# A searched task order replaced by another one in a fused delta-rule attention and gated FFN kernel

## The chip, the core and the metric

The kernel runs on one core of one Trainium2 chip. The metric is the device time of one launch in microseconds (us). PE is TensorE, which multiplies matrices; DVE is VectorE, ACT is ScalarE, POOL is GpSimd, SP is SyncE. SP and ACT also issue DMA transfers, each to a queue of its own (q1 and q10 in the profile).

## What is computed

The reference is a delta-rule recurrence over 768 steps for 4 batches and 8 heads of width 48, and behind it a gated FFN on the 3072 tokens that it gives:

```python
for t in range(S):
    y[:, :, t] = einsum('bhd,bhde->bhe', q[:, :, t], state)
    v_old = einsum('bhde,bhd->bhe', state, k_n[:, :, t])
    state = state + bt * einsum('bhd,bhe->bhde', k_n[:, :, t], vt - v_old)
h = x @ w_in          # (3072, 384) @ (384, 2048)
out = (h * cos(h)) @ w_out
```

All data is 32-bit float; `k_n` is `k` over its norm.

## The kernel before

**Units.** The 768 steps are cut into 24 units of 32 steps (`unit(n)`, L1492). A unit turns its keys and queries (`turn`, L635), multiplies them into Gram matrices (`gram`, L662), inverts a triangular matrix, reads the state (`through_state`, L915, task `state`), solves (`solve`, L984), updates the state (`update`, L1019), adds what lies within the unit (`within`, L1037), and transposes the result into FFN features (`features`, L1070). Each of these is a run of small matmuls on PE with a copy, product or sum on DVE or ACT behind it (`turn_out`, `gram_keys`, `right_side`, `solve_out`, `update_out`, `within_out`, `features_out`). The state chains unit to unit.

**Inverses.** For units 0 and 1 the inverse is made by doubling (`doubling`, L1463): six levels of small matmuls on PE for each of two parities (`double(n, level, par)`, L749), with a transpose, a sum or a copy on DVE or ACT between levels. Units 2 and up go in pairs `m = n // 2`: the Gram matrix is written to DRAM (`gram_put`), read back in another layout (`gram_get`), inverted column by column on POOL (`invert`, L867, seven tasks `inv(m, 0..6)`, five shorter ones for `m = 1`, of which the first runs on DVE), written again (`put`) and read back (`get`). A `get` of units 2 and 3 is eight transfers (L900), a later one four (L908).

**FFN.** Two units make a pass `p` of 256 tokens. Passes 0 and 1 run plain: eight blocks `hidden(p, f)` (L1092) and eight output blocks `out(p, i, k)` (L1292) on PE. Passes 2 to 11 run a scheme with fewer products: 20 `layer` blocks (L1267) and 14 `out` blocks (L1349) each. The weights come as 28 transfers (`weights(t)`) and pass ACT (`split`), DVE (`shift`) and POOL (`add`) before PE can use them: `hidden(0, 0)` needs `add` 0 to 2, `hidden(0, 6)` up to 11, `out(0, 0, k)` up to `add` 15 + 4k.

**Filler.** `keep_warm` (L491) is one matmul on constants whose result nothing reads. Five run ahead of everything (`WARM_FIRST`), `WARMS` more are tasks of the order. Once `out(0, 0, 0)` has been issued, L492 lets the rest issue nothing.

**The order.** Every piece is a task, given to `order.add` with its engine, its predecessors and the buffers that it takes and gives back. `Order.LINE` (L101) is one fixed sequence over all tasks, by number in the order in which they were added; `Order.run` (L219) emits them in that sequence and hands out buffers as it goes. Each engine runs its own tasks strictly in this order (L1904 to L1910), and the transfers of SP and ACT are issued in this order across both queues (L1911 to L1915). The set `Order.OTHER` (L62) picks, task by task, the other queue (L375) or the other engine (L378): a transfer in the set goes to ACT's queue and not to SP's; an `x_sum` or `inv` in it runs on DVE and not on POOL, and a `left`, `right` or `in_sums` in it on POOL and not on DVE.

Of the kernel before, what the change touches and what calls it, by code (L numbers as in the profile page):

```python
# [59 lines left out]
class Order:  # L60

    OTHER = {  # L62
        ('gram_put', 2), ('q', 3), ('gram_get', 1), ('inv', 1, 0), ('put', 1), ('gram_put',
        4), ('gram_put', 5), ('v', 7), ('v', 8), ('v', 9), ('blocks', 11, 1), ('gram_put',
        11), ('put', 5), ('v', 13), ('put', 6), ('gram_put', 15), ('gram_get', 7), ('get',
        15), ('v', 16), ('blocks', 16, 0), ('blocks', 16, 1), ('gram_put', 16), ('blocks',
        18, 1), ('k', 19), ('blocks', 19, 0), ('gram_get', 9), ('get', 19), ('gram_put',
        20), ('v', 21), ('gram_put', 21), ('put', 10), ('gram_put', 22), ('v', 23),
        ('gram_put', 23), ('gram_get', 11), ('right', 4, 4), ('left', 1, 1, 0), ('left', 1,
        3, 0), ('left', 1, 3, 1), ('store', 1, 0), ('x_sum', 2, 'd'), ('x_sum', 2, 'n'),  # L70
        ('x_sum', 2, 'm'), ('x_sum', 2, 'e'), ('x_sum', 2, 'k'), ('x_sum', 2, 'g'),
        ('x_sum', 2, 'i'), ('x_sum', 2, 'l'), ('x_sum', 2, 'f'), ('x_sum', 2, 'b0'),
        ('left', 2, 4, 1), ('left', 2, 3, 1), ('x_sum', 3, 'd'), ('x_sum', 3, 'n'),
        ('x_sum', 3, 'm'), ('x_sum', 3, 'e'), ('x_sum', 3, 'k'), ('x_sum', 3, 'g'),
        ('x_sum', 3, 'i'), ('x_sum', 3, 'l'), ('x_sum', 3, 'h'), ('x_sum', 3, 'b0'),
        ('left', 3, 4, 1), ('left', 3, 3, 1), ('x_sum', 4, 'd'), ('x_sum', 4, 'm'),
        ('x_sum', 4, 'g'), ('x_sum', 4, 'i'), ('left', 4, 3, 0), ('left', 4, 3, 1),
        ('store', 4, 0), ('x_sum', 5, 'd'), ('x_sum', 5, 'e'), ('x_sum', 5, 'l'), ('x_sum',
        5, 'h'), ('x_sum', 5, 'b0'), ('left', 5, 2, 0), ('left', 5, 4, 1), ('left', 5, 3,
        0), ('left', 5, 3, 1), ('store', 5, 0), ('x_sum', 6, 'd'), ('x_sum', 6, 'g'),  # L80
        ('x_sum', 6, 'l'), ('x_sum', 6, 'f'), ('x_sum', 6, 'b0'), ('left', 6, 1, 0),
        ('left', 6, 4, 0), ('store', 6, 1), ('x_sum', 7, 'd'), ('x_sum', 7, 'm'), ('x_sum',
        7, 'g'), ('x_sum', 7, 'i'), ('x_sum', 7, 'f'), ('x_sum', 7, 'h'), ('x_sum', 7,
        'b0'), ('left', 7, 4, 0), ('left', 7, 4, 1), ('left', 7, 3, 1), ('x_sum', 8, 'd'),
        ('x_sum', 8, 'm'), ('x_sum', 8, 'e'), ('x_sum', 8, 'k'), ('x_sum', 8, 'g'),
        ('x_sum', 8, 'l'), ('left', 8, 3, 0), ('store', 8, 0), ('store', 8, 1), ('x_sum', 9,
        'd'), ('x_sum', 9, 'm'), ('x_sum', 9, 'e'), ('x_sum', 9, 'k'), ('x_sum', 9, 'i'),
        ('x_sum', 9, 'l'), ('x_sum', 9, 'b0'), ('left', 9, 1, 0), ('left', 9, 2, 0),
        ('left', 9, 1, 1), ('left', 9, 3, 0), ('store', 9, 0), ('x_sum', 10, 'k'), ('x_sum',
        10, 'i'), ('x_sum', 10, 'l'), ('x_sum', 10, 'h'), ('x_sum', 10, 'b0'), ('left', 10,  # L90
        1, 0), ('left', 10, 1, 1), ('left', 10, 4, 1), ('left', 10, 3, 0), ('left', 10, 3,
        1), ('store', 10, 0), ('x_sum', 11, 'd'), ('x_sum', 11, 'e'), ('x_sum', 11, 'k'),
        ('x_sum', 11, 'g'), ('x_sum', 11, 'f'), ('left', 11, 1, 0), ('left', 11, 2, 0),
        ('left', 11, 1, 1), ('left', 11, 3, 0), ('left', 11, 3, 1), ('store', 11, 1),
        ('store_right', 11), ('weights', 5), ('weights', 7), ('weights', 15), ('weights',
        16), ('weights', 18), ('weights', 20), ('weights', 22), ('weights', 23), ('weights',
        25), ('weights', 27)
    }

    WARM_FIRST, WARMS = 5, 56  # L100
    LINE = """  # L101
# [1845 lines left out]
```

## Time and profile before

| what | us |
|---|---|
| three timed runs | 638.47, 639.97, 640.19 (median 639.97) |
| profiled execution: span, first to last instruction | 636.6 |
| median of the runs less that span | 3.4 |
| PE busy, all instructions | 619.2 |
| of it `keep_warm` (L493) | 23.1 |
| DVE / ACT / POOL busy | 495.1 / 297.7 / 435.8 |

The profiled execution has no timer of its own beside its span; what lies around the span is taken to be the 3.4 us of the table. PE's records come in two per matmul (one per transpose), each with its load of the stationary operand (PEld). The profile tells by "issue" that an engine waited for nothing that the trace shows. The queue q8 carries PE's instructions in packets of 16 KB.

### The profile page before, as it was taken

The numbers are of one execution on the slowest core, as the hardware profiler recorded it, in microseconds if no ns is written. First come the engines' busy times: TensorE is split into PE (matmuls) and PEld (weight loads), VectorE is DVE, ScalarE is ACT, GpSimd is POOL, SyncE is SP. The second block draws the span as 40 slices with busy tenths as digits, with TensorE's granted clock in tenths as the row PEclk, the third lists the DMA queues.
The fourth block names the chain that finished last, engine by engine and source line by source line (L and its number), as shares of the span: only waits on it lengthen the run. The fifth ranks groups of instructions, "written<-read, shape, count | busy, mean of one in ns | idle before, by whom it ended". The sixth has DMA issues, their size and how long they took to land.

```text
span 636.6 us, 24189 instructions
## 1 busy us (share of the span) xinstructions
PE 619.2 (97%) x10176; PEld 576.2 (90%) x10176; DVE 495.1 (78%) x1030; ACT 297.7 (47%) x528; POOL 435.8 (68%) x780
## 2 busy tenths in 40 slices
PE   5999989999999999999999999999999999999997
PEld 4877877987899999999999999999999999999997
DVE  5776656779998999887898888888888776566682
ACT  3457556562423444643642644733643553545440
POOL 5247788678788788887789888886884883112241
PEclk8899999999999999999999999999999999999999
DMA  8978656563651555435435344333304102000001
GB/s 173 221 171 213 121 155 146 93 118 60 116 68 22 94 90 99 60 67 104 61 70 98 56 73 90 58 57 67 74 3 81 44 1 43 19 2 26 1 25 26
DMA packets 209381, 50.37 MB, mean 79 GB/s; under 512 B 200920, under 2 KB 204280, under 8 KB 209272
## 3 DMA queue, kind: packets, MB, share of 16 engines
q1 hardware_dynamic: 161896, 35.03, 29.3%
q10 hardware_dynamic: 47072, 13.25, 10.0%
q8 instruction: 80, 1.31, 0.9%
q0 software_dynamic: 304, 0.54, 0.4%
q14 instruction: 29, 0.24, 0.1%
HBM read 38.55 MB, written 10.22 MB: 77 GB/s over the span
## 4 chain that ended last, share of the span: by engine, by line
PE 90%; DVE 3%; DMA 3%; ACT 1%; issue 1%; POOL 0%; SPq 0%; ACTq 0%; DVEq 0%
PE p_out L1353 29%; PE p_h L1271 27%; PE p_h L1097 6%; PE p_kq L928 4%; PE p_out L1295 3%; PE p_s L1025 3%; PE p_g L673 3%; PE p_h L757 3%; PE p_kq L1055 3%; PE p_u L1000 3%; PE p_out L493 2%; PE p_h L1353 2%; PE p_z L1076 1%; DMA kp<-in_k_dram 1%; PE p_t L640 1%
## 5 line engine op out<-in xcount | busy, mean ns | idle before, releaser
L877 POOL TENSOR_TENSOR part<-z,gb 128x126 f32<-128x126 f32 (+23 forms) x321 | 144.6, 451 | 46.7 <-DMA gb<-g_dr 21.2
L884 POOL TENSOR_TENSOR z<-z,part 128x126 f32<-128x126 f32 (+23 forms) x321 | 145.5, 453 | 25.1
L1353 PE MATMUL p_out<-w_out,g_ffn 128*128 128x192 f32 x672 | 121.9, 328 | 0.3 <-DVE o L1405 0.2
L1353 PEld LDWEIGHTS p_out<-w_out,g_ffn 128*128 128x128 f32 x672 | 107.7, 190 | 1.7 <-DVE o L1405 0.7
L1150 ACT ACTIVATE turns<-turns,halfpi 128x512 f32<-128x512 f32 x96 | 68.0, 719 | 55.7 <-DVE turns L1141 42.6
L1353 PE MATMUL p_out<-w_sum,g_ffn 128*128 128x192 f32 x496 | 89.7, 329 | 0.2 <-DVE o L1405 0.2
L1271 PE MATMUL p_h<-x_sum,w_in 128*128 128x128 f32 x640 | 84.0, 277 | 0.0
L1134 ACT ACTIVATE turns<-g_ffn,quarter_turn 128x512 int32<-128x512 f32 x70 | 49.8, 719 | 66.4 <-DVE g_ffn L1288 31.3
L1353 PEld LDWEIGHTS p_out<-w_sum,g_ffn 128*128 128x128 f32 x496 | 79.6, 190 | 1.2 <-issue 0.4
L1271 PEld LDWEIGHTS p_h<-x_sum,w_in 128*128 128x128 f32 x640 | 78.8, 192 | 1.1
L1288 DVE TENSOR_TENSOR g_ffn<-g_ffn,p_h 128x512 f32<-128x512 f32 x80 | 54.3, 681 | 17.3 <-PE p_h L1271 16.4
L1141 DVE SCALAR_TENSOR_TENSOR turns<-g_ffn,turns 128x512 f32<-128x512 f32 x70 | 55.3, 796 | 13.1 <-ACT turns L1134 13.0
L1068 ACT COPY y<-p_kq 32x384 f32<-32x384 f32 x96 | 45.2, 470 | 30.4 <-PE p_kq L1055 22.5
L1153 DVE TENSOR_TENSOR g_ffn<-turns,g_ffn 128x512 f32<-128x512 f32 x70 | 51.5, 745 | 3.8 <-ACT turns L1150 3.7
L1271 PE MATMUL p_h<-x_sum,in_sum 128*128 128x128 f32 x400 | 52.9, 277 | 0.0
L572 POOL TENSOR_TENSOR knrm<-ksum,halves 128x16 f32<-128x16 f32 (+1 forms) x14 | 36.4, 2602 | 23.9 <-DMA qp<-in_q_dram 12.6
L1271 PEld LDWEIGHTS p_h<-x_sum,in_sum 128*128 128x128 f32 x400 | 49.7, 192 | 0.8
L1405 DVE SCALAR_TENSOR_TENSOR o<-p_out,o 128x192 f32<-128x192 f32 x74 | 25.1, 351 | 28.4 <-PE p_out L1353 28.0
L1097 PE MATMUL p_h<-x_ffn,w_in 128*128 128x128 f32 x384 | 45.8, 277 | 0.0
L1097 PEld LDWEIGHTS p_h<-x_ffn,w_in 128*128 128x128 f32 x384 | 44.1, 192 | 1.2
L1271 PE MATMUL p_h<-x_ffn,w_in 128*128 128x128 f32 x320 | 42.4, 277 | 0.0
L1369 POOL TENSOR_TENSOR g_ffn<-g_ffn,g_ffn 128x512 f32<-128x512 f32 x18 | 25.8, 1442 | 22.5 <-PE p_out L1353 18.7
(168 smaller groups left out, 1071.3 us busy)
## 6 DMA issues: line engine op xcount, KB each, us to landing
g_ffn<-in_moe_w_in_dram SPq DMA_DIRECT2D x10, 512.0 KB
gb<-g_dr SPq DMA_DIRECT2D x14, 256.0 KB
vp<-in_v_dram SPq DMA_DIRECT2D x68, 48.0 KB
g_ffn<-in_moe_w_out_dram SPq DMA_DIRECT2D x8, 384.0 KB
g_ffn<-in_moe_w_out_dram ACTq DMA_DIRECT2D x8, 384.0 KB
kp<-in_k_dram SPq DMA_DIRECT2D x120, 24.0 KB
out_dram<-o SPq DMA_DIRECT2D x14, 192.0 KB
zt<-z_dr SPq DMA_DIRECT2D x72, 32.0 KB
```

What stands on the lines that cost most here:

```text
L572: nc.gpsimd.tensor_tensor(out=scales[m][2][:, part], in0=sums[m, part.start][:, 0:n], in1=halves[:, 0:n], op=ALU.pow,)
L877: eng.tensor_tensor(out=part, in0=z[:, 0:rows, j, None].to_broadcast(shape), in1=a[:, j, None, j + 1 :].to_broadcast(shape), op=ALU.mult,)
L884: eng.tensor_tensor(out=behind, in0=behind, in1=part, op=ALU.subtract)
L1068: nc.scalar.copy(by_parity(y[quarter(b)]), p_kq[quarter(b ^ 1), :, b % 2])
L1097: nc.tensor.matmul(p_h[:, i], w_in[:, t, (4 * k + i) * 128 : (4 * k + i + 1) * 128], xts[p][:, t, unit * 128 : (unit + 1) * 128], start=(i ...
L1134: nc.scalar.activation(turns[p, f], hidden_of(p, f), AF.Identity, bias=quarter_turn, scale=TURN)
L1141: nc.vector.scalar_tensor_tensor(out=r, in0=hidden_of(p, f), scalar=TURN, in1=t, op0=ALU.mult, op1=ALU.subtract,)
L1150: nc.scalar.activation(r, r, AF.Sin, bias=halfpi, scale=2.0 * math.pi)
L1153: nc.vector.tensor_tensor(out=place(p, f), in0=step_of(rests.pop((p, f)), f), in1=step_of(hidden_of(p, f), f), op=ALU.mult,)
L1271: nc.tensor.matmul(p_h[:, e], in_block(*w)[:, e], x_of(p, b), start=new and e == 0, stop=True, skip_group_check=True,)
L1288: nc.vector.tensor_tensor(out=part_of(p, to), in0=part_of(p, one), in1=part_of(p, two), op=op)
L1353: nc.tensor.matmul(p_o, left(p, part, a)[:, e % 4], right(e, b), start=(e == 0), stop=(e == FT // 2 - 1), skip_group_check=True,)
```

## The change

Nothing of the work changes but its order. Three things are replaced:

```diff
     OTHER = {
-        ('gram_put', 2), ('q', 3), ('gram_get', 1), ('inv', 1, 0), ('put', 1), ('gram_put',
...
+        ('q', 3), ('v', 3), ('inv', 1, 0), ('gram_put', 5), ('gram_get', 2), ('put', 2),
...
     }
-    WARM_FIRST, WARMS = 5, 56
+    WARM_FIRST, WARMS = 5, 14
     LINE = """
-0 1 66 2 70 2084 3 71 4 8 9 72 122 67 68 5 2085 123 69 127 73 128 124 65 75 125 80 76 77 2088 178 78
...
+0 24 1 25 136 8 2 3 5 26 27 28 29 30 31 33 2042 80 81 32 4 85 86 139 137 2046 165 9 10 11 12 2050
...
```

`LINE` is new from its first row to its last. With 42 `warm` tasks fewer, a task numbered 64 or more before has a number lower by 42 after. In `OTHER`, the entries of the attention's transfers (`q`, `k`, `v`, `blocks`, `gram_put`, `gram_get`, `put`, `get`) go from 34 to 25, those of `store` from 9 to 6, those of `weights` from 10 to 11, and they are largely other ones; all `x_sum`, `left`, `right` and `inv` entries stay. So no computation changes its engine, and some transfers change between SP's and ACT's queue.

The head of PE's order, decoded (w is a `warm`, d a `double(n, level, par)`, h a `hidden`):

```
before: turn0 w w gram0 turn1 d001 d000 gram1 w d010 d100 w w d011 d110 w w w d020 w w
  d021 d101 turn2 w w d111 turn3 d030 d031 w gram2 w d120 w w d041 w w gram3 d040 w w
  d121 d050 d051 turn4 w solve0 d130 w update0 w within0 d131 d140 w features0 state1 turn5
  d141 gram4 h(0,0) d151 d150 w w solve1 w update1 within1 gram5 w h(0,2) features1 state2
  turn6 h(0,4) solve_half2 w between2 w solve2 h(0,6) update2 w within2 gram6 h(0,8)
  features2 state3 turn7 h(0,10) solve_half3 between3 solve3 out(0,0,0) h(0,12) update3
  within3 h(0,14) out(0,0,1) features3 state4 gram7 h(1,0) h(1,2) h(1,4) h(1,6) out(0,0,2)
  h(1,8) solve4
after:  w turn0 gram0 turn1 w w w w turn2 d001 d000 gram1 w w w w d101 d011 d010 gram2 d021
  d111 d020 d031 d121 turn3 d030 d100 gram3 d110 d041 d040 d131 d050 turn4 d051 d141 d120
  solve0 d130 update0 within0 d151 d140 features0 state1 d150 h(0,0) turn5 h(0,2) solve1
  update1 within1 gram4 h(0,4) gram5 state2 features1 h(0,6) turn6 h(0,8) solve_half2
  between2 out(0,0,0) solve2 update2 within2 h(0,10) state3 gram6 h(0,12) solve_half3
  between3 solve3 out(0,0,1) turn7 out(0,0,2) update3 h(0,14) features2 within3 gram7 h(1,0)
  state4 features3 h(1,2) h(1,4) h(1,6) solve4
```

The head of the order of transfers, without the first sixteen, of `k` and `q` (a = ACT's queue):

```
before: weights0 v0 weights1 k2 weights2 k3 weights3 q2 weights4 a:q3 a:weights5 k4 weights6
  v1 q4 a:weights7 k5 weights8 q5 ... a:put1 q6 a:weights16 a:gram_put5 get2 gram_get2
after:  k2 weights0 q2 weights1 k3 a:weights2 weights3 v0 weights4 k4 a:weights5 a:q3 weights6
  v1 weights7 q4 weights8 k5 a:weights9 ... put1 q6 weights17 gram_put4 weights18
  a:gram_put5 get2 weights19 a:gram_get2
```

DVE's tasks follow the same pattern: before, unit 1's doubling has three of its six levels behind it in each parity when `solve(0)` is issued; after, five levels in parity 1 and three in parity 0, and four products are left where there were six.

More of the change, by code (lines that the diff above doesn't have):

```diff
@@ L62 @@
     OTHER = {
-        ('gram_put', 2), ('q', 3), ('gram_get', 1), ('inv', 1, 0), ('put', 1), ('gram_put',
[L64 to L97, printed above, removed]
+        ('q', 3), ('v', 3), ('inv', 1, 0), ('gram_put', 5), ('gram_get', 2), ('put', 2),
+        ('get', 8), ('gram_put', 9), ('v', 10), ('gram_put', 10), ('put', 5), ('blocks', 15, 0),
@@ new lines @@
+        ('gram_put', 15), ('gram_get', 7), ('v', 16), ('gram_get', 8), ('v', 18), ('v', 19),
+        ('blocks', 19, 0), ('blocks', 20, 0), ('blocks', 20, 1), ('blocks', 22, 0),
+        ('blocks', 22, 1), ('gram_put', 22), ('gram_put', 23), ('get', 23), ('right', 4, 4),
+        ('left', 1, 1, 0), ('left', 1, 3, 0), ('left', 1, 3, 1), ('x_sum', 2, 'd'),
+        ('x_sum', 2, 'n'), ('x_sum', 2, 'm'), ('x_sum', 2, 'e'), ('x_sum', 2, 'k'),
+        ('x_sum', 2, 'g'), ('x_sum', 2, 'i'), ('x_sum', 2, 'l'), ('x_sum', 2, 'f'),
@@ new lines @@
+        ('x_sum', 2, 'b0'), ('left', 2, 4, 1), ('left', 2, 3, 1), ('x_sum', 3, 'd'),
+        ('x_sum', 3, 'n'), ('x_sum', 3, 'm'), ('x_sum', 3, 'e'), ('x_sum', 3, 'k'),
+        ('x_sum', 3, 'g'), ('x_sum', 3, 'i'), ('x_sum', 3, 'l'), ('x_sum', 3, 'h'),
+        ('x_sum', 3, 'b0'), ('left', 3, 4, 1), ('left', 3, 3, 1), ('store', 3, 1),
+        ('x_sum', 4, 'd'), ('x_sum', 4, 'm'), ('x_sum', 4, 'g'), ('x_sum', 4, 'i'),
+        ('left', 4, 3, 0), ('left', 4, 3, 1), ('store', 4, 1), ('x_sum', 5, 'd'),
@@ new lines @@
+        ('x_sum', 5, 'e'), ('x_sum', 5, 'l'), ('x_sum', 5, 'h'), ('x_sum', 5, 'b0'),
+        ('left', 5, 2, 0), ('left', 5, 4, 1), ('left', 5, 3, 0), ('left', 5, 3, 1),
+        ('x_sum', 6, 'd'), ('x_sum', 6, 'g'), ('x_sum', 6, 'l'), ('x_sum', 6, 'f'),
+        ('x_sum', 6, 'b0'), ('left', 6, 1, 0), ('left', 6, 4, 0), ('store', 6, 1),
+        ('x_sum', 7, 'd'), ('x_sum', 7, 'm'), ('x_sum', 7, 'g'), ('x_sum', 7, 'i'),
+        ('x_sum', 7, 'f'), ('x_sum', 7, 'h'), ('x_sum', 7, 'b0'), ('left', 7, 4, 0),
@@ new lines @@
+        ('left', 7, 4, 1), ('left', 7, 3, 1), ('x_sum', 8, 'd'), ('x_sum', 8, 'm'),
+        ('x_sum', 8, 'e'), ('x_sum', 8, 'k'), ('x_sum', 8, 'g'), ('x_sum', 8, 'l'),
+        ('left', 8, 3, 0), ('x_sum', 9, 'd'), ('x_sum', 9, 'm'), ('x_sum', 9, 'e'),
+        ('x_sum', 9, 'k'), ('x_sum', 9, 'i'), ('x_sum', 9, 'l'), ('x_sum', 9, 'b0'),
+        ('left', 9, 1, 0), ('left', 9, 2, 0), ('left', 9, 1, 1), ('left', 9, 3, 0),
+        ('store', 9, 0), ('x_sum', 10, 'k'), ('x_sum', 10, 'i'), ('x_sum', 10, 'l'),
```

8 lines of the change are left out of this document (added), and 196 rows, old and new, of the table LINE.

## The prediction

> **What bounds the kernel now.** The page first, then the busy time by stretch. The page's rows: the span, PE's share, PE's busy tenths in 40 slices, and the queue that carries PE's instructions.
>
> ```profile
> span 636.6 us, 24189 instructions
> PE 619.2 (97%) x10176; PEld 576.2 (90%) x10176; DVE 495.1 (78%) x1030; ACT 297.7 (47%) x528; POOL 435.8 (68%) x780
> ...
> PE   5999989999999999999999999999999999999997
> ...
> q8 instruction: 80, 1.31, 0.9%
> ```
>
> PE is the bound, but 97% hides filler. The stretches (columns: length; busy PE, PEld, DVE, ACT, POOL; clock, DMA, GB/s) are cut at events of TensorE's order:
>
> ```profile
> 14.83:45.78 30.95, 30.89 (x541) 25.12 (x542) 24.56 (x76) 14.16 (x29) 10.48 (x7) 0.90 0.84 184
> 45.78:59.05 13.27, 11.43 (x310) 9.05 (x308) 9.42 (x30) 9.05 (x19) 9.60 (x13) 1.00 0.85 230
> 59.05:79.23 20.18, 19.20 (x418) 17.34 (x412) 13.09 (x26) 13.16 (x27) 15.70 (x23) 1.00 0.67 143
> 79.23:104.64 25.41, 22.39 (x643) 18.86 (x643) 14.18 (x32) 13.47 (x26) 22.08 (x47) 1.00 0.57 147
> 104.64:632.96 528.32, 527.30 (x8184) 499.68 (x8182) 425.42 (x842) 242.27 (x419) 369.23 (x676) 1.00 0.34 61
> ```
>
> From 104.64 on PE idles 1.02 us in 528: no order of the same work can win there, it can only lose. Before, PE looks busy as well, but with what? The groups of PE between 21.3 and 104.6 us show the filler:
>
> ```profile
> L493 PE MATMUL p_out<-o 128*128 128x256 f32 x56 | 17.0, 411 | 0.0
> ```
>
> So 17 us of that stretch are matmuls that nobody reads, in places where the real work waited. The milestones of PE in the start (start, length, line, count) and behind:
>
> ```profile
> 14.88 1.97 PE L757 MATMUL p_h<-in_sum 64*64 64x64 f32 x32 [2.95 <-DVE in_sum L722]
> 33.55 1.15 PE L757 MATMUL p_h<-in_sum 64*64 64x64 f32 x32
> 47.09 1.14 PE L1000 MATMUL p_u<-vp,in_sum 64*64 64x48 f32 x32 [0.73 <-ACT kq_t L650]
> 54.45 0.55 PE L1076 MATMUL p_z<-consts,y 128*128 128x128 f32 x3 [0.46 <-ACT y L1068]
> 59.05 2.94 PE L1097 MATMUL p_h<-x_ffn,w_in 128*128 128x128 f32 x24
> 61.92 1.15 PE L757 MATMUL p_h<-w_sum 64*64 64x64 f32 x32
> ```
>
> ```profile
> 66.41 0.89 PE L1025 MATMUL p_s<-u,kp 64*64 64x96 f32 x32 [0.59 <-DVE u L1012]
> 68.54 0.86 PE L673 MATMUL p_g<-kq_t 48*32 48x64 f32 x64
> 79.89 0.88 PE L958 MATMUL p_v<-g_ffn,in_sum 32*32 32x48 f32 x64
> 81.45 0.86 PE L994 MATMUL p_u<-g_ffn,w_sum 32*32 32x48 f32 x59
> 83.87 0.28 PE L994 MATMUL p_u<-g_ffn,w_sum 32*32 32x48 f32 x5 [1.56 <-issue]
> 92.79 0.49 PE L1076 MATMUL p_z<-consts,y 128*128 128x128 f32 x3
> 101.14 0.88 PE L994 MATMUL p_u<-g_ffn,w_sum 32*32 32x48 f32 x64 [0.73 <-DVE g_ffn L978]
> ```
>
> **What the packets cost now.** 10176 matmul records and as many weight loads in 80 packets are 254 instructions each. One run of 64 small matmuls is 128 instructions in 0.8 us (79.89 to 80.70), so two runs eat a packet in under 2 us. The order puts a packet's end inside `solve(2)`, where 59 of 64 matmuls run and 1.56 us are lost on nothing that the trace names. In the window 80.9 to 82.4 us the queues show the packet that was missing, behind q1's transfers:
>
> ```profile
> q8 instruction: 1, 0.02, 5.6%
> ```
>
> From 79.89, when the packet before it was begun, to 83.87 are 3.98 us. A second place is like it, 201.23 to 204.44, 3.2 us:
>
> ```profile
> 201.23 0.86 PE L673 MATMUL p_g<-kq_t 48*32 48x64 f32 x64
> 204.44 0.27 PE L673 MATMUL p_g<-kq_t 48*32 48x64 f32 x2 [0.49 <-issue]
> ```
>
> So a packet whose work takes PE under 3.2 to 4.0 us stalls it. Together that cost 2.05 us. [...]
>
> **The change, step by step.** 22 of the 36 fillers that ran go (31 tasks before `out(0,0,0)` become 9). Alone that is worth nothing: they lay in waits. What counts is when real work can start.
>
> *Step 1, the first FFN block.* Its inputs hang on unit 0: from `solve(0)` (47.09) to `features(0)` (54.45) are 7.4 us, a chain of DVE, PE and ACT. Before, PE then does `state(1)`, `turn(5)`, a double and `gram(4)` and reaches `hidden(0,0)` at 59.05; after, only `state(1)` and a double lie between, 1.7 us. `solve(0)` needs unit 0's doubling, and that is DVE's. Two of DVE's groups between 12 and 62 us (busy, mean ns, idle before):
>
> ```profile
> L777 DVE TENSOR_TENSOR in_sum<-in_sum,p_h 128x256 f32<-128x256 f32 x8 | 3.1, 407 | 0.7 <-PE p_h L757 0.6
> L773 DVE STREAM_TRANSPOSE in_sum<-p_h 128x256 f32<-128x256 f32 x6 | 2.5, 432 | 1.4 <-PE p_h L757 1.4
> ```
>
> After, DVE's list from 14.83 to the last sum of unit 0 has 14 such transposes and 12 such sums (10.9 us by 432 and 407 ns) and about 18.6 us of other tasks by their durations in the same stretch: 29.5 us, against 24.56 before to the same event, as more of unit 1 stands ahead of it. If DVE never idled, `solve(0)` would start at 45.8 (14.83 + 29.5, and 1.5 for a wait on the norms and a double ahead of it in PE's order) and `hidden(0,0)` at 45.8 + 7.4 + 1.7 + about 0.2 = 55.1. If DVE idled as now (24.56 busy of 30.95, 79%), the 29.5 us would take 37.2, and `hidden(0,0)` would come at 62. I take 56.5: the two units' products alternate in the new list, so most of its waits fall under the other unit's work. In it is 0.5 us for `turn(2)`, which now stands ahead of the first double and needs `q2`, third in the order of transfers where it was seventh; such a set of four takes SP 1.8 us or more:
>
> ```profile
> 65.60 1.80 SPq L396 DMA_DIRECT2D qp<-in_q_dram  x4
> ```
>
> **Gain 2.5 us, bounds 3.9 and -3.0.**
>
> *Step 2, up to unit 2.* PE's work from `hidden(0,0)` to `solve_half(2)` after: five FFN blocks by 2.87 (59.05 to 61.92), two turns, two grams, one each of solve, update, within, state, features: about 20.7 us; and 1.9 for what PE waits on DVE's u and the update, now 0.59 (66.41) and fillers. That would put `solve_half(2)` at 79.1. But `get(2)` is now queued behind `gram_put(5)`, which follows `gram(5)`, about 15 us behind `hidden(0,0)`, at 71.5. SP's rows:
>
> ```profile
> 68.38 6.50 SPq L900 DMA_DIRECT2D w_sum<-z_dr  x8
> 74.97 1.75 SPq L852 DMA_DIRECT2D gb<-g_dr  x2
> ```
>
> `gram(5)` to `get(2)`'s issue: about 1.5 us; the issue 6.5 (half of it may be a wait that is gone by then); landing 0 to 3.5 us behind it (PE took it at 78.35 before, without a wait). I take `solve_half(2)` at 81.0, a wait of 1.9 that was not there. From there to the end of `gram(6)`: 4.6 us of work, 0.65 and 1.2 us of waits on the halves and on u (`out(0,0,0)` covers the third), and 0.8 for packets (below): 88.2, with `out(0,0,0)`'s 2.6 us done besides. Before, the same set is done when `hidden(0,8)` ends, 92.7. **Lead 4.5 us.** Before, 1.56 (packet) and three fillers went here.
>
> *Step 3, unit 3 and pass 1.* The half solves wait as before (0.73 at 101.14). New: `out(0,0,2)` stands ahead of `update(3)` now and needs POOL's `add` 22 and 23 behind `inv(2,3)`, 0 to 1, I take 0.3; and `solve(4)` needs pair 2's inverse:
>
> ```profile
> 81.26 0.23 POOL L877 TENSOR_TENSOR part<-z,gb 128x31 f32<-128x31 f32 x1
> 114.67 0.23 POOL L884 TENSOR_TENSOR z<-z,part 128x16 f32<-128x16 f32 x1
> 122.07 0.53 SPq L889 DMA_DIRECT2D z_dr<-z  x1
> 132.87 1.25 PE L1000 MATMUL p_u<-rhs,zt 64*64 64x48 f32 x32
> ```
>
> 33.6 us on POOL, then 7.4 to the `put` and 10.8 to the solve. After, `gram_get(2)` is issued behind `get(2)`, about 3 us later than at 74.97, so the inverse ends near 118; PE wants `solve(4)` at 132.87 less the lead of 4.5 and the block of 2.87 that no longer stands ahead of it, 125.5. The `put`, `get` and landings took 18.2 with other transfers between, of which some 8 are their own: a wait of 0 to 2.5, I take 1.0. **Lead left 3.2.**
>
> *Step 4, the saturated rest.* Kinds of blocks that follow each other are counted the same within a few; the distances from `state` to `solve`, `solve` to `update`, `update` to `state` in PE's work are as long as before or longer. What differs are packets. In the new order the work in one packet is below 3.3 us in six places behind the doubling (2.67 and 2.76 near 71 and 88 us, 3.25 twice, 2.94, 2.74), against three before (1.93, 3.14, 2.67). At 3.2 to 4.0 us each place costs 0 to 1.3; the first two and one 3.25 are in step 2's 0.8. For the other three I take 1.0, less the 0.49 that goes: **-0.5.**
>
> Sum: 3.2 - 0.5 = 2.7 us. 636.6 - 2.7 = 633.9 of span, and with the 3.4 us around it 637.3, against the median 639.97.
>
> **The clock.** It is the one price of the missing filler. PE's busy time in stretches as the clock record cuts them (length, busy PE, clock):
>
> ```profile
> 7.64:11.05 3.41, 1.78 (x71) 1.00 1.03 240
> 11.05:14.47 3.42, 0.88 (x5) 0.50 0.74 187
> 17.88:21.29 3.41, 3.41 (x34) 0.50 1.05 239
> 21.29:24.71 3.42, 3.42 (x49) 1.00 0.96 217
> 45.19:48.60 3.41, 2.68 (x57) 1.00 0.91 307
> ```
>
> A stretch with 52% busy was followed by half clock, until one that was full; 79% kept it. After, without filler from `double(1,0,1)` on, PE's real work fills 65 to 80% of 22 to 55 us. [...]
>
> **Rivals.** (a) *The lead is given back* at `solve(4)` or in packets: both at their upper ends, 2.7 - 1.5 - 1.5 = -0.3: 640.3, between 638.1 and 641.9. For it: the inverse of pair 2 is one chain, moved later. Against: one FFN block less stands before that solve. Packets that do no better than before are part of this. (b) *DVE idles as it does now*: from 79% the first FFN block comes at 62, 5.5 us later than taken, and all behind it: 642.8, slower. It decides at 59 for `hidden(0,0)`. For it: 33.98 us busy of 44.2 up to 59.05 before. Against: the interleaved list. (c) *The clock falls* between 22 and 55 us: a pair of doubles takes 1.97 at half clock (14.88) and 1.15 at full (33.55). 21 doubles by 0.41 and turns and grams are some 10 us, of which DVE's list hides half, and the first FFN blocks lose 1 to 2 till the clock is back: 6.5 us, 643.8, slower. It decides at a busy share between 52 and 79%.
>
> **How the numbers follow.** Forecast 0.47 (631 to 638), (a) 0.21, (b) 0.17, (c) 0.15. A measurement here tells 0.3%, 1.9 us, from no change: faster is under 638.05, slower over 641.9. Faster 0.47, within 0.3% 0.21, slower 0.32. The range: step 1 at its best and no wait in steps 2 and 3 give 631; (b) and (c) reach 644 and a little over: 631 to 645.
>
> **What would show it.** Right: `hidden(0,0)` between 55 and 58; `hidden(0,8)` done before 81; no more than 1.5 us of PE idle behind 130 us; clock 1.00 from 21.3 on. Step 2 is wrong if `solve_half(2)` waits for nothing or for more than 4 us; step 4 if "issue" ahead of PE exceeds 3 us in all. The forecast fails if PE's first FFN block comes after 59, or if a transfer in pass 2 or later holds up DVE's list and PE with it, which no row of before shows.

## The result, and the profile after

The changed kernel takes 646.36 us (median of 4 runs, 644.53 to 649.53) against 639.22 for the kernel before (median of 4): ratio 1.0115, 95% interval 1.0091 to 1.0139. It is 7 us slower. The profiled execution took 647.02, of which 645.2 is span. The page of the changed kernel, rows as shown of before:

```profile
span 645.2 us, 24082 instructions
PE 616.3 (96%) x10132; PEld 575.8 (89%) x10132; DVE 491.3 (76%) x1030; ACT 296.8 (46%) x528; POOL 426.6 (66%) x780
...
PE   7778888997999999999999999999999999999997
...
PEclk7998899999899999999999999999999999999999
```

In PE's digits the tenth slice (145 to 161 us) is a 7 where before had a 9; the 7s and 8s of the first seven slices stand where the filler that is gone filled waits. The clock's row has 8s in the fourth, fifth and eleventh slice, where the forecast had it at 1.00. The windows of the prediction, for the changed kernel, and three cut where its clock was at half (columns as before):

```profile
14.83:45.78 30.95, 25.18 (x574) 21.07 (x573) 25.73 (x81) 16.77 (x35) 11.75 (x12) 0.98 0.84 220
45.78:59.05 13.27, 10.40 (x231) 9.70 (x228) 11.80 (x31) 8.06 (x16) 12.09 (x13) 0.87 0.66 168
59.05:79.23 20.18, 17.08 (x367) 16.24 (x366) 13.65 (x27) 13.58 (x27) 14.74 (x25) 0.88 0.70 164
79.23:104.64 25.41, 22.19 (x643) 19.41 (x641) 13.91 (x29) 13.69 (x27) 20.32 (x42) 0.96 0.55 134
104.64:632.96 528.32, 521.85 (x8183) 492.20 (x8184) 416.95 (x837) 239.83 (x416) 359.76 (x679) 0.99 0.35 61
53.82:57.24 3.42, 3.42 (x78) 3.30 (x70) 2.18 (x9) 2.74 (x6) 3.42 (x3) 0.50 1.00 223
74.30:81.13 6.83, 6.32 (x40) 6.23 (x40) 6.10 (x9) 3.50 (x8) 6.13 (x6) 0.50 0.63 144
159.64:166.46 6.82, 5.65 (x71) 3.46 (x72) 4.96 (x13) 3.02 (x5) 3.99 (x6) 0.50 0.82 119
```

The part from 104.64 us on, which could only lose, lost: PE idles 6.5 us there instead of 1.0. And the clock, at half once before (11 to 21 us), is at half three more times. The timeline of PE shows the places. First the early one:

```profile
55.97 3.54 PE L1094 MATMUL p_h<-x_ffn,w_in 128*128 128x128 f32 x24
...
71.91 1.01 PE L925 MATMUL p_kq<-st,kq_t 48*64 48x48 f32 x51
74.81 0.67 PE L925 MATMUL p_kq<-st,kq_t 48*64 48x48 f32 x13 [1.88 <-issue]
75.41 0.90 PE L1073 MATMUL p_z<-consts,y 128*128 128x128 f32 x3
76.10 5.24 PE L1094 MATMUL p_h<-x_ffn,w_in 128*128 128x128 f32 x24
...
84.83 0.88 PE L955 MATMUL p_w<-rhs,w_sum 32*32 32x48 f32 x64
```

`hidden(0,0)` starts at 55.97, 3.1 us ahead of before. At 72.9 PE stops inside `state(2)` and waits for nothing that the trace names, as it did inside `solve(2)` before; experiment 3 shows that the place moves with the count of instructions, so it is taken to be a packet (q8 moves one between 72.4 and 73.6 us). Then the clock halves (0.50 from 74.30 to 81.13 us) and `hidden(0,6)` takes 5.24 us instead of 2.9, and the last row, `solve_half(2)`, comes at 84.83, with no wait of its own. The late place, in PE's timeline and in the longest wait of PE from 130 us on (the other three are 1.2 us together):

```profile
154.75 0.49 PE L1073 MATMUL p_z<-consts,y 128*128 128x128 f32 x3
155.17 1.15 PE L925 MATMUL p_kq<-st,kq_t 48*64 48x48 f32 x64
160.81 1.18 PE L670 MATMUL p_g<-kq_t 48*32 48x64 f32 x64 [4.49 <-ACT x_ffn L1081]
161.92 4.21 PE L1292 MATMUL p_out<-w_out,g_ffn 128*128 128x384 f32 x6
```

```profile
PE p_g L670 <- ACT x_ffn L1081: 4.5, 1, 4.5
```

`gram(9)` waits 4.5 us for a PSUM bank that ACT's `features_out(5)` (L1081) empties, though `features(5)` was done at 155.2. ACT's timeline says why; first the changed kernel, then the kernel before, whose line numbers are higher by 3:

```profile
151.73 1.92 ACT L1065 COPY y<-p_kq 32x384 f32<-32x384 f32 x4
159.41 0.84 ACT L552 ACTIVATE g_ffn<-kp 128x768 f32<-128x768 f32 x1 [5.75 <-DMA qp<-in_q_dram]
160.28 0.48 ACT L1081 COPY x_ffn<-p_z 128x384 f32<-128x384 f32 x1
```

```profile
154.39 0.48 ACT L1084 COPY x_ffn<-p_z 128x384 f32<-128x384 f32 x1 [1.16 <-PE p_z L1076]
...
161.60 0.84 ACT L555 ACTIVATE g_ffn<-kp 128x768 f32<-128x768 f32 x1 [1.01 <-DVE g_ffn L1153]
```

ACT sits 5.75 us in front of `square(6,0)`, the squares of keys 12 and 13, until a transfer lands (the row names one of `q`; the task itself needs `k(12)` and `k(13)`), and the 0.48 us copy that PE needs stands behind it. In the kernel before, the square comes seven microseconds after the copy. SP's timeline has the transfers: `k(13)` is one task of eight issues, and SP is never free ahead of it.

```profile
147.48 2.03 SPq L412 DMA_DIRECT2D qp<-in_q_dram  x4
149.60 1.92 SPq L393 DMA_DIRECT2D vp<-in_v_dram  x4
151.62 4.65 SPq L393 DMA_DIRECT2D kp<-in_k_dram  x8
```

To follow where time is won and lost, the experiments below use one number: the **lead**, the real work of PE done by a time (fillers left out, each task counted at the shortest duration that the compared profiles show for it), less what the kernel before had done by then. In the changed kernel's profile it is 2.9 us at 50 us, 3.5 at 70, 0.1 at 80, 2.3 at 85, 0.1 at 105, -0.1 at 155, -6.8 at 165 and -8.3 at 175; behind that it drifts to -9.7 at 620. It is good to about 1 us: the spans differ by 8.6 us where it says 9.7.

**Theory A**: the loss is made between 150 and 190 us, by tasks in the lists of ACT and SP that wait for transfers and stand ahead of tasks that feed PE. **Rivals**: the early packets and the clock lose it; the missing filler loses it; the choice of queues loses it; the lead is owed by other engines and is given back under any order.

### The profile page after: what moved, and what is told of

Read it like the earlier page. It is cut to its first block, busy times and chain, and to the rows that moved or that the text cites. A ratio compares the mean times of both kernels' runs of the same rounds, so it can differ in the third digit from the quotient of the medians.

```text
span 645.2 us, 24082 instructions
## 1 busy us (share of the span) xinstructions
PE 616.3 (96%) x10132; PEld 575.8 (89%) x10132; DVE 491.3 (76%) x1030; ACT 296.8 (46%) x528; POOL 426.6 (66%) x780
## 4 chain that ended last, share of the span: by engine, by line
PE 71%; POOL 11%; DMA 6%; DVE 5%; issue 3%; ACT 2%; SPq 1%; ACTq 0%; POOLq 0%; DVEq 0%
PE p_out L1350 22%; PE p_h L1268 22%; PE p_h L1094 6%; POOL z L881 5%; POOL part L874 4%; PE p_out L1292 4%; PE p_kq L925 3%; PE p_s L1022 2%; PE p_kq L1052 2%; PE p_u L997 2%; PE p_g L670 2%; DMA kp<-in_k_dram 2%; PE p_h L1350 2%; DMA qp<-in_q_dram 1%; PE p_h L754 1%
## 5 line engine op out<-in xcount | busy, mean ns | idle before, releaser
L881 POOL TENSOR_TENSOR z<-z,part 128x126 f32<-128x126 f32 (+23 forms) x321 | 144.0, 449 | 25.1
L874 POOL TENSOR_TENSOR part<-z,gb 128x126 f32<-128x126 f32 (+23 forms) x321 | 137.2, 427 | 34.8 <-DMA gb<-g_dr 6.6
L1350 PE MATMUL p_out<-w_sum,g_ffn 128*128 128x192 f32 x496 | 88.1, 327 | 0.0
L1268 PE MATMUL p_h<-x_sum,w_in 128*128 128x128 f32 x640 | 84.8, 278 | 0.4 <-DVE g_ffn L1285 0.4
L1150 DVE TENSOR_TENSOR g_ffn<-turns,g_ffn 128x512 f32<-128x512 f32 x70 | 54.0, 776 | 12.1 <-ACT turns L1147 11.9
L1138 DVE SCALAR_TENSOR_TENSOR turns<-g_ffn,turns 128x512 f32<-128x512 f32 x70 | 52.9, 764 | 12.7 <-ACT turns L1131 12.7
L1268 PE MATMUL p_h<-x_sum,in_sum 128*128 128x128 f32 x400 | 54.2, 280 | 0.0
L1094 PE MATMUL p_h<-x_ffn,w_in 128*128 128x128 f32 x384 | 49.1, 288 | 0.0
L1094 PEld LDWEIGHTS p_h<-x_ffn,w_in 128*128 128x128 f32 x384 | 47.0, 203 | 0.8
L1268 PE MATMUL p_h<-x_ffn,w_in 128*128 128x128 f32 x320 | 42.8, 277 | 0.0
```

The source lines that it names most:

```text
L874: eng.tensor_tensor(out=part, in0=z[:, 0:rows, j, None].to_broadcast(shape), in1=a[:, j, None, j + 1 :].to_broadcast(shape), op=ALU.mult,)
L881: eng.tensor_tensor(out=behind, in0=behind, in1=part, op=ALU.subtract)
L1094: nc.tensor.matmul(p_h[:, i], w_in[:, t, (4 * k + i) * 128 : (4 * k + i + 1) * 128], xts[p][:, t, unit * 128 : (unit + 1) * 128], start=(i ...
L1138: nc.vector.scalar_tensor_tensor(out=r, in0=hidden_of(p, f), scalar=TURN, in1=t, op0=ALU.mult, op1=ALU.subtract,)
L1150: nc.vector.tensor_tensor(out=place(p, f), in0=step_of(rests.pop((p, f)), f), in1=step_of(hidden_of(p, f), f), op=ALU.mult,)
L1268: nc.tensor.matmul(p_h[:, e], in_block(*w)[:, e], x_of(p, b), start=new and e == 0, stop=True, skip_group_check=True,)
```

## The experiments

Each lists its edit by task names; all are moves in `LINE` or entries of `OTHER`. The table has the medians, the ratio to the kernel before with its interval, and the lead of the one profile at 130 and 190 us. The runs come from several chips, each with its own runs of the kernel before (medians 637.98 to 639.38), so what differs between groups (1 to 4, 5 to 8, 9 to 11, 12 and 13, 14 to 16) is read from the ratios.

| | us (runs) | ratio | lead 130 | lead 190 |
|---|---|---|---|---|
| changed kernel | 646.36 (4) | 1.0115 [1.0091, 1.0139] | 0.0 | -7.6 |
| 1 square late | 643.40 (6) | 1.0091 [1.0066, 1.0116] | 5.4 | -2.9 |
| 2 before, square early | 643.93 (6) | 1.0091 [1.0070, 1.0112] | -0.8 | -5.0 |
| 3 hidden ahead | 644.57 (6) | 1.0096 [1.0066, 1.0125] | 2.0 | -4.3 |
| 4 both (1 and 3) | 644.46 (5) | 1.0092 [1.0069, 1.0115] | 3.1 | -4.1 |
| 5 square and sum late | 643.61 (6) | 1.0066 [1.0047, 1.0085] | 1.7 | -5.9 |
| 6 and get(6) ahead | 640.17 (12) | 1.0022 [1.0004, 1.0039] | 1.8 | -2.3 |
| 7 and hidden ahead | 642.20 (12) | 1.0057 [1.0038, 1.0076] | 4.5 | -2.2 |
| 8 before, less filler | 638.25 (12) | 0.9986 [0.9966, 1.0007] | 2.8 | 3.0 |
| 9 ACT's list | 642.79 (10) | 1.0050 [1.0027, 1.0073] | -1.9 | -7.6 |
| 10 after, queues of before | 655.18 (4) | 1.0268 [1.0249, 1.0287] | 5.0 | -1.0 |
| 11 before, queues of after | 647.68 (6) | 1.0142 [1.0112, 1.0172] | 1.2 | 0.5 |
| 12 v by ACT | 643.11 (12) | 1.0063 [1.0034, 1.0092] | 4.5 | -1.2 |
| 13 get(6) alone | 643.15 (8) | 1.0092 [1.0057, 1.0127] | 6.6 | -0.1 |
| 14 after's head, before's rest | 637.10 (12) | 0.9968 [0.9941, 0.9995] | -1.2 | -2.9 |
| 15 before's head, after's rest | 653.11 (6) | 1.0222 [1.0197, 1.0247] | -2.9 | -15.8 |
| 16 as 14, hidden ahead | 637.00 (12) | 0.9988 [0.9964, 1.0012] | 3.4 | 2.4 |

**1. The square behind the copy.**

```diff
-within_out(5) right(1,6) square(6,0) gram_keys(8) ... features_out(5) blocks(10,0) turns(1,14)
+within_out(5) right(1,6) gram_keys(8) ... features_out(5) square(6,0) blocks(10,0) turns(1,14)
```

> The changed kernel with one task of its order moved: square(6,0), the squares of keys 12 and 13 on ScalarE, goes from seven tasks ahead of features_out(5) to just behind it. Theory A: in the changed kernel ScalarE sits 5.75 us in front of that square until a transfer lands, features_out(5) stands behind it in ScalarE's list, and gram(9) on TensorE waits 4.5 us for the bank that features_out(5) empties; the half clock from 159.6 to 166.5 us follows from that hole (out(0,1,1) 5.08 instead of 2.74 us, and part of the next block). So the wait ahead of gram(9) falls below 0.3 us, the record of half clock at 160 is gone, and the time falls from 646.4 to 637.5 to 640. Rival B: keys 13 are late for more than this; the wait moves to the next task that needs them or to turns(1,14), and the time stays at 642 to 645. Rival C: the loss is spread over the whole order and the time stays within 1 us of 646.4.

The hole ahead of `gram(9)` is gone, but the time is 643.40, in the range of rival B. Against the kernel before the ratio fell from 1.0115 to 1.0091, some 1.5 us, and the two intervals overlap, so by the time alone this one move gains nothing that is certain. The longest waits of PE, then of DVE, in that kernel from 150 to 180 us:

```profile
PE p_u L997 <- DMA zt<-z_dr: 2.8, 1, 2.8
PE p_h L1268 <- DVE g_ffn L1150: 1.8, 1, 1.8
```

```profile
DVE turns L1138 <- ACT turns L1131: 3.5, 1, 3.5
```

The square still holds `turns(1,14)` behind it, DVE waits 3.5 us for that, PE for DVE; then `solve(6)` meets `get(6)`, which is not there. This profile entered with a lead of 5.4 us, since its `state(2)` had no hole, and left with -2.9.

**2. The kernel before with the square early.**

```diff
-features(5) features_out(5) weigh(3) ... v(9) sum(5,0) right(2,4) k(13) ... square(6,0)
+features(5) k(13) square(6,0) features_out(5) weigh(3) ... v(9) sum(5,0) right(2,4)
```

> The kernel before with the changed kernel's order at that one place: keys 13 are loaded and squared (square(6,0)) ahead of features_out(5) instead of behind it; two tasks are moved, nothing else. Theory A: features_out(5) on ScalarE, which ran at 154.4 us, waits behind the square until keys 13 have landed (issued from about 150.5, some 5 us of issuing on SP's queue, 2 to 3 us to landing), so to 158 to 160 us; TensorE, at gram(8), waits about 4 us for the bank, the clock halves for about 7 us behind it, and the time goes from 639.2 to 644 to 648. Rival B (keys and square as such cost nothing in the order before, because TensorE has other work to do): under 641. Rival C (the loss of the changed kernel is spread): within 1 us of 639.2.

0.9% slower, just under 644. ACT and PE in its profile:

```profile
157.26 0.84 ACT L555 ACTIVATE g_ffn<-kp 128x768 f32<-128x768 f32 x1 [3.34 <-DMA kp<-in_k_dram]
...
158.12 0.48 ACT L1084 COPY x_ffn<-p_z 128x384 f32<-128x384 f32 x1
```

```profile
158.66 1.18 PE L673 MATMUL p_g<-kq_t 48*32 48x64 f32 x64 [2.54 <-ACT x_ffn L1084]
```

A hole of 2.5 us and half clock from 158.5 to 161.9, and the lead falls from -0.8 to -5.0. These two moves alone make a good kernel lose 0.9%, 6 us, of which 4.2 show in the stretch. Theory A's wait is real; its price was a little over-sized (2.5 instead of 4 us).

**3 and 4. hidden(0,6) ahead of state(2), alone and with 1.**

```diff
-gram(5) ... state(2) weigh(1) ... features(1) hidden(0,6) turn(6)
+gram(5) ... hidden(0,6) state(2) weigh(1) ... features(1) turn(6)
```

> The changed kernel with one task moved: hidden(0,6), 2.7 us of TensorE with no wait ahead of it, goes from behind features(1) to ahead of state(2). Theory A (the instruction packet): between the boundary at which the packet was asked for (69.9 us) and the next lie then about 5.2 us of TensorE's work instead of 2.9, so the 2.1 us hole inside state(2) and the half clock from 74.3 to 81.1 us (hidden(0,6) took 5.08 instead of 2.74 us) go, and solve_half(2) starts at 80.5 to 82 instead of 84.8. Whether that reaches the end: Theory A1, the 3 to 4 us are kept, time 642 to 643.5; Rival A2, they are given back by 105 us to waits that come after (solve(2) to update(2) 1.2 us, gram(6) 0.6, between(3) and solve(3) 1.4), since both orders had done equal work by 105 us, and the time stays within 1 us of 646.4.

> Both single moves: square(6,0) behind features_out(5), hidden(0,6) ahead of state(2). If the two act alone and both reach the end: 634 to 637, below the kernel before. If the early one is given back by 105 us: the time of the first experiment, 637.5 to 640. If neither matters: 646.

In 3 the hole in `state(2)` shrinks to 0.5 us, and it moves:

```profile
75.41 0.79 PE L925 MATMUL p_kq<-st,kq_t 48*64 48x48 f32 x37 [0.54 <-issue]
```

37 of the 64 matmuls are left behind it where 13 were. The difference is 24, the records of the `hidden(0,6)` that now stands ahead, so the place goes by the count of instructions, as the end of a packet would. In 4, 7 and 16 the hole is gone; in the third `solve_half(2)` starts at 82.6, in the fourth at 80.5. But neither median is distinguishable from its partner (644.57 against 646.36, 644.46 against 643.40), and neither meets a time that its text names: nothing shows that the early hole costs the median.

**5 and 6. Further down ACT's and SP's lists.**

```diff
-square(6,0) ... features_out(5) ... turns(1,14) ... sum(6,0) ... gate(1,14) ... blocks(11,1) ... get(6)
+features_out(5) ... turns(1,14) square(6,0) ... gate(1,14) sum(6,0) ... get(6) blocks(11,1)
```

The fifth moves `square(6,0)` and `sum(6,0)`, the sixth `get(6)` too.

> The changed kernel with square(6,0) moved further down ScalarE's list, behind turns(1,14) as well, and sum(6,0), which needs it, behind gate(1,14) on VectorE. In the first experiment the bank came free in time, but the square still stood ahead of turns(1,14), VectorE sat 3.5 us in front of rest(1,14), and TensorE lost 1.8 us ahead of layer(2,15) and then 2.8 us ahead of solve(6), which waited for the transfer get(6). Theory A (ScalarE's list holds the other engines up): the hole of 1.8 us goes as well, and if get(6) moves up with VectorE the time is 638 to 641. Rival B (SP's list is what sets solve(6): get(6) stands behind the loads of blocks(11,1) and store(0,0)): the wait ahead of solve(6) takes over what was won, 2.8 to 4.5 us, and the time stays at 642 to 644.

> The kernel of the fifth experiment (square(6,0) and sum(6,0) late) and get(6) moved ahead of blocks(11,1) in SP's list, four tasks. In the first experiment SP issued blocks(11,1) from 163.0 to 165.2 and store(0,0) to 165.9 us ahead of get(6), put(3) having been issued at 160.6. Rival B: get(6) is issued about 2.9 us earlier and the 2.8 us ahead of solve(6) go; together with the moves in the lists of ScalarE and VectorE nothing of more than 1 us is left between 155 and 175 us, and the time is 636.5 to 640. If the loss there belongs to the amount of work on VectorE and not to these lists: 642 to 644 as before.

The waits of PE between 148 and 192 us, first in the fifth, then in the sixth:

```profile
PE p_u L997 <- DMA zt<-z_dr: 2.6, 1, 2.6
PE p_h L1268 <- DVE x_sum L1183: 1.7, 1, 1.7
```

```profile
PE p_h L1268 <- DVE x_sum L1183: 1.8, 1, 1.8
PE p_h L1268 <- ACT p_h L1280: 1.4, 1, 1.4
```

Rival B of the fifth was right (SP's list sets `solve(6)`), and with `get(6)` moved the 2.6 us are gone. Three tasks moved, and 0.9% of the 1.15% is back: 640.17, just above the 636.5 to 640 that was expected. The intervals of 5, 7 and 9 end just below where the changed kernel's begins, the sixth's far below. It still has two holes of over 1 us there, so the expectation that nothing of the kind would be left was wrong.

**7. The same with hidden(0,6) ahead.**

> The sixth experiment and hidden(0,6) ahead of state(2) as in the third. If the lead from the first 100 us is kept once the holes between 155 and 175 us are closed: 634 to 638, that is at or below the kernel before. If VectorE or the transfers cap it: the time of the sixth experiment within 1 us.

642.20, not better than the sixth but 0.3% worse. It enters with 4.5 us and leaves the stretch with the same -2.2 as the sixth, which entered with 1.8; then `solve(12)` at 301.8 waits 2.3 us for its `get`, with half clock behind it. An early lead did not help, and the time lies in neither of the expected ranges.

**8. The kernel before with 14 fillers.**

```diff
-        if not out_begun:
+        if not out_begun and (warmed.append(1) or len(warmed) <= 14):
```

> The kernel before, its order as it is, but its fillers on TensorE stop after the first 14 (5 ahead, 9 in the order), so that as many run as in the changed kernel; 22 of 36 go. Filler computes nothing that is used. Theory C (the missing filler costs the clock, whatever the order): half clock falls on some stretch between 22 and 81 us, 2 to 4 us, so 641 to 643. Theory A (the order, not the filler): the clock record stays at full from about 21 us or halves only where TensorE does not set the time, and the time stays within 1.5 us of the kernel before.

Same time within the interval, although the clock does fall in its profile, from 62.4 to 65.8 us, where it is full in the kernel before. So with the order of before the missing filler does not cost the time, and its rival falls there; experiment 14 has as little filler with the changed head, and is not slower than the kernel before either.

**9. square(6,0) and gram_put(9) behind the cosines.**

```diff
-turns(1,14) square(6,0) ... gram_put(9) ... cos(1,14) ... cos(1,12) gate(1,12)
+turns(1,14) ... cos(1,14) ... cos(1,12) square(6,0) gram_put(9) gate(1,12)
```

> The seventh experiment with ScalarE's list mended further: square(6,0) and gram_put(9), a transfer that ScalarE issues, go behind cos(1,14) and cos(1,12). In the seventh ScalarE sat 4.2 us in front of the square (keys 13), then some 3 us in front of the first of the three issues of gram_put(9), and VectorE waited 5.8 us for the cosine behind them, TensorE 2.7 us at layer(2,15). Theory A (tasks of ScalarE that wait for transfers stand ahead of tasks that feed VectorE and TensorE, and this is what the stretch from 155 to 180 us costs): that hole of 2.7 us goes, the loss against the kernel before between 155 and 185 us falls from 7.0 (fourth and seventh) and 4.3 (sixth) to 3 us or less, and the time is 635.5 to 639. Rival B (VectorE's list as a whole is late there): the wait ahead of layer(2,4) for x_sum, 1.7 us, grows by what was won, and the time is 640 to 643.

The hole at `layer(2,15)` went, one of 2.7 us at `layer(2,9)` took its place, and the stretch cost 5.7 us. The time is in the range of rival B, but not by its mechanism: `layer(2,4)` waits for nothing now.

**10 and 11. The queues exchanged.** Only the set `OTHER` changes sides.

> The changed kernel's order with the queues of the kernel before: the set OTHER is put back, the order is untouched, so v(7), v(8), v(9) and others are issued by ScalarE again and gram_put(9), gram_put(10) by SP. SP has some 4 us less to issue ahead of keys 13. If the queues made the loss: 638 to 640. If the order made it (theory A), keys 13 land 2 to 4 us earlier, square(6,0) still stands ahead of features_out(5), and part of the hole ahead of gram(9) stays: 641 to 645.

> The kernel before with the changed kernel's set OTHER, its order untouched. If the queues made the loss: 644 to 647. If the order made it: within 2 us of the kernel before, since keys 13 are squared there only at 161.6 us, after the tasks that feed TensorE, and SP's later issues have that much room.

Both are worse than the kernel before, by 16 and 9 us (the tenth is also some 9 us above the changed kernel), and both expectations failed on the time. But the stretch tells order from queue. PE's busy time from 150 to 190 us in the tenth, then in the eleventh:

```profile
150.00:190.00 40.00, 36.25 (x670) 31.10 (x668) 31.80 (x70) 12.90 (x24) 32.36 (x65) 0.96 0.47 76
```

```profile
150.00:190.00 40.00, 40.00 (x662) 34.14 (x650) 35.51 (x71) 13.22 (x25) 31.82 (x59) 1.00 0.54 87
```

The changed order loses there with the old queues (lead 5.0 to -1.0), the old order loses nothing with the new ones. But the queues choose which wait it is. In the tenth, PE's waits from 148 to 192 us:

```profile
PE p_u L998 <- DMA zt<-z_dr: 3.2, 2, 3.0
PE p_g L671 <- ACT x_ffn L1082: 0.5, 1, 0.5
```

The hole ahead of `gram(9)` is down to 0.5 us, and `solve(6)` waits for its `get` instead. What the exchange costs comes later, where transfers meet an order that they were not placed for; in the eleventh, PE's longest wait from 190 us on:

```profile
PE p_u L999 <- DMA zt<-z_dr: 3.2, 3, 2.3
```

**12. v(7), v(8) by ACT, gram_put(9) by SP, on top of 6; and 13, get(6) ahead alone, on top of the changed kernel.**

> The sixth experiment (square(6,0), sum(6,0) late, get(6) ahead) with three loads on the other queue: v(7) and v(8) are issued by ScalarE, as in the kernel before, and gram_put(9) by SP, as there. SP issued 65 transfers in 34.6 us between 125 and 165 us in the changed kernel, 51 in 29.1 us in the kernel before. Theory A' (what is left between 155 and 185 us comes from who issues the loads: keys 13 land late behind SP's other issues, and gram_put(9) stands in ScalarE's list ahead of the cosines): keys 13 are issued 3 to 4 us earlier, the holes at layer(2,4) (1.8 us) and layer(2,9) (1.4 us) fall below 0.5, and the time is 636 to 639. Rival B (the order alone): the time of the sixth experiment within 1 us, 639.2 to 641.2; or above it, if ScalarE's own list suffers from the four issues of each v, 641 to 643.

> The changed kernel with get(6) ahead of blocks(11,1) in SP's list and nothing else. Theory A (waits in series): in the changed kernel solve(6) does not wait at all, it stands behind the hole ahead of gram(9); the move alone gives under 1 us, 645 to 647, and gave 3.4 us behind the moved square only because the square's hole was gone. Rival (the two are separate costs that add up): 3.4 us as there, 642 to 643.5.

The twelfth did not gain (its holes: 1.1 us at `solve(6)`, 2.4 at `layer(2,9)`), so A' is not borne out. The thirteenth is undecided: its runs spread from 639 to 649, its interval takes in both expectations (without the two runs near 649 the median is 642.0, nearer to the rival's). Its one profile, of the fastest run, still has the hole, and nothing else:

```profile
PE p_g L670 <- ACT x_ffn L1081: 4.7, 1, 4.7
```

**14, 15, 16. Heads and rests exchanged.** `LINE` is one kernel's up to `solve(4)`, near 130 us, then the other's; a transfer goes with its place.

```diff
-after: [after's tasks to solve(4)] [after's tasks behind]
+14:    [after's tasks to solve(4)] [before's tasks behind]
+15:    [before's tasks to solve(4)] [after's tasks behind]
```

> The changed kernel's order up to solve(4), about 130 us, and behind it the rest in the order of the kernel before; each transfer is issued by the queue of the kernel from which its place comes. At that place the two orders differ by 8 tasks done earlier and 7 done later. Theory A (the loss lies between 150 and 190 us and belongs to the changed order's second part): up to solve(4) TensorE leads as in the six profiles that share the changed kernel's first 140 us, -0.1 to 6.7 us, mean 3.3; behind it nothing is lost, as nothing is in the kernel before; time 634.5 to 637.5. Rival D (the lead is owed to work that the other engines have not done, so any second part gives it back): the lead goes between 150 and 190 us and the time is 638 to 640. Rival B (a kernel of its own timing, whose transfers land at the wrong places, as with the exchanged queues): 643 or more.

> The other way round: the order of the kernel before up to solve(4) and the changed kernel's order behind it. Theory A: no lead at 130 us, then 6 to 8 us lost between 150 and 190 us at gram(9) and behind it, with half clock there; time 644 to 648. If the loss belonged to the first part or to the way the parts meet: under 641.

> The kernel of the fourteenth experiment with hidden(0,6) ahead of state(2) as in the third. Of the six profiles that share the changed kernel's first 140 us four show a hole inside state(2) (1.5 to 3.5 us) and the half clock behind it, of the three with hidden(0,6) moved ahead none shows the hole. Theory (the packet at state(2) and the clock behind it take 1 to 5 us from the lead in the runs in which they come): median 0.5 to 2 us below the fourteenth experiment and a smaller spread, 633.5 to 636. Rival: within 0.7 us of the fourteenth, since waits up to 105 us take the lead anyway.

(Four of six, in the last text, is a miscount: `state(2)` has a hole of over 1 us in three of those six profiles, 1.2, 1.9 and 3.0 us, and of 1.6 us in the fourteenth; of the three with `hidden(0,6)` ahead, the third has one of 0.5.) The stretch in the kernel before, the changed one, the fourteenth and the fifteenth:

```profile
150.00:190.00 40.00, 40.00 (x688) 34.06 (x678) 36.12 (x71) 13.11 (x25) 32.49 (x59) 1.00 0.54 88
```

```profile
150.00:190.00 40.00, 35.51 (x672) 29.67 (x672) 30.00 (x67) 14.20 (x27) 29.97 (x58) 0.91 0.52 81
```

```profile
150.00:190.00 40.00, 39.92 (x660) 32.92 (x659) 34.59 (x69) 13.48 (x25) 30.26 (x55) 1.00 0.54 88
```

```profile
150.00:190.00 40.00, 34.55 (x554) 28.49 (x553) 29.55 (x60) 11.82 (x21) 35.30 (x68) 0.87 0.51 81
```

This settles the place. With the changed head and the old rest PE stays busy, the time is 637.10, and the kernel is 0.3% faster than before (interval 0.9941 to 0.9995; the sixteenth's takes in 1, so the gain is just at the edge of the noise). Its profile is of one of its slower runs, 640.69. With the old head and the changed rest the lead falls by 12.9 us from 130 to 190, more than theory A's 6 to 8, and the time is 653.11, above the expected range; why it is more than under the changed head is not shown. The sixteenth's profile shows that a lead need not be given back under a good rest (3.4 at 130, 2.2 at 620), against the rival of the owed lead; its median equals the fourteenth's, so the packet at `state(2)` is once more not seen in the median.

## Why the prediction was wrong

The forecast was 637.3 us, 2.7 less than before; the time is 646.36, some 7 us more, and above the 645 at which the range ended. The step that failed is the fourth. (What lies around the span is 1.8 us, 647.02 less 645.2, and not 3.4; the rest of the 3.4 is that the profiled execution of before ran below the median. The forecast difference does not hang on it.)

**Step 1** came out: `hidden(0,0)` at 55.97, forecast 56.5; rival (b), 62, falls. In part that is luck: `solve(0)` came at 45.1, 2.1 us ahead of what the forecast implies (56.5 less 9.3), and from there it took 10.9 us to `hidden(0,0)` and not 9.3, the last two of them at half clock. DVE is busy for 25.73 of the 30.95 us, 83%.

**Steps 2 and 3** came near in the mean, 2.7 us of lead where 3.2 was forecast, but by luck: their new waits did not come. The sum has 1.9 us ahead of `solve_half(2)`, for `get(2)`, and 1.0 us ahead of `solve(4)`, for the inverse of pair 2. Seven profiles share the changed head and its queues to about 125 us (changed, 1, 5, 6, 12, 13, 14), and in none does PE wait at either place; the prediction itself names a `solve_half(2)` that waits for nothing as the sign that step 2 is wrong. What came instead is the half clock: `solve_half(2)`, forecast at 81.0, starts at 78.1 and 78.8 in the two profiles without it between 20 and 105 us, and at 81.0 to 84.8 in the five with it. The waits of 0.65 and 1.2 us behind it were right (0.65 and 1.24). `gram(6)` ended at 99.1, not 88.2, and 6.5 us of this are `out(0,0,0)`, `hidden(0,10)` and `state(3)`, which stand ahead of it and are not in the 4.6 us of work; the lead does not change by this, since their work is left out with their time.

The leads of the seven at 130 us are 0.0, 5.4, 1.7, 1.8, 4.5, 6.6 and -1.2. Roughly, they fall with the half clock between 20 and 105 us: none in 1 and 13, 3.4 us in 12, 6.8 in 5 and 14, 10.2 in 6 and the changed kernel. The packet that was given 0.8 us in the sum is a hole of 0 to 3.0 us in `state(2)`, and in the changed kernel and in the fifth experiment 6.8 us at half clock follow it.

**Step 4, the saturated rest, failed.** It said that the distances in PE's order are "as long as before or longer" and that "what differs are packets", for 0.5 us. It compared PE's list with itself, and put the lists of the other engines at nothing without a reason. What moved was ACT's list (`square(6,0)` ahead of `features_out(5)`, `turns(1,14)` and, behind them, `gram_put(9)` ahead of two cosines) and SP's (`get(6)` behind `blocks(11,1)`). The changed rest costs 4 to 8 us between 130 and 190 us in every profile that has the changed head (and 12.9 in the fifteenth); the old rest costs 0 to 2. "No more than 1.5 us of PE idle behind 130 us" was about 6; "clock 1.00 from 21.3 on" was three times false; "issue" stayed at 2.8 (1.88, 0.41 and 0.48 us at three places), under the bound of 3; that a packet with under 3.2 to 4.0 us of work stalls PE was the author's estimate from two holes of the kernel before. The named condition of failure, a transfer in pass 2 or later that holds up a list, came true one engine over: ACT's, not DVE's, at the change from pass 1 to pass 2.

**The clock**, rival (c), is not what made the loss. In the changed kernel's profile it is full from 22 to 53.8 us and falls to half later, three times, behind windows in which PE had idled; with the same start it did fall between 22 and 55 us in the profiles of 4 (6.8 us) and 6 (10.2), and 6 is the best of the mends. Less filler did not cost the time in 8 or 14. The clock's records in the profiles of the kernel before and the changed one have 1.00 and 0.50 alone, so the granted clock of each run gives its time at half clock, twice the missing share times the span (24.5 us for the changed kernel's 0.981 in 645.2, and 24.8 by its records): medians 21 us in the changed kernel's runs, 7.6 in the 97 runs of the kernel before beside the experiments and in the sixth. In the fourteenth the eight runs with 10.2 us or less took 634.1 to 637.2, the four with 11.5 to 24.4 took 639.5 to 643.5. Where half clock follows a hole, their shares are not separated by an experiment. In the changed kernel's profile the first six records of `out(0,1,1)` take 4.21 us at half clock; all eight of `out(0,0,3)` took 2.85 in the kernel before.

Left open: which of the waits in the stretch is worth how much. The mends 1, 5, 7, 9 and 12 each closed a hole and found the next one, and their intervals overlap; only the exchange of the whole rest left none above 1 us.

## What to carry to other kernels

When an order is replaced, compare it on every engine, not only on the one that bounds the kernel: for each task that waits for a transfer, list what now stands behind it in its own engine's list and who waits for that. A wait of a cheap engine that PE meets can be paid again as half clock: in the second experiment 2.54 us of wait came with 3.4 us at half clock. And one profile of such a start is a draw: seven profiles of the same head, with holes of 0 to 3.0 us in `state(2)`, spread over 8 us of lead, so a mean over profiles, or an exchange of halves, decides what a single trace can't.

## What was not expected of the hardware

The clock changes in steps of 3.41 us (its records at half last 3.41, 6.83 or 10.24 us, but for the one at the end of each run), and what it does next goes here with PE's busy share in the 3.41 us before, a window below. Three windows of the changed kernel at full clock, each followed by half clock (51%, 60% and 3% busy):

```profile
50.40:53.82 3.42, 1.76 (x53) 1.35 (x51) 3.29 (x8) 3.23 (x7) 3.42 (x3) 1.00 0.53 177
70.88:74.30 3.42, 2.05 (x118) 1.72 (x118) 1.80 (x5) 1.50 (x4) 1.45 (x2) 1.00 1.09 285
156.22:159.64 3.42, 0.10 (x8) 0.00 (x0) 0.00 (x0) 0.23 (x1) 2.72 (x10) 1.00 0.37 51
```

Over all profiles here, behind 18 us and at full clock: all 16 windows with PE under 46% busy were followed by half clock; of those between 47 and 69%, 16 were and 84 were not; of 3075 above 69%, none. So PE need not be idle for a whole window: the second of the three above has 1.4 us of the 1.88 us hole in `state(2)` in it and no other idle time. What decides between 47 and 69% is not shown.
